# All loads of a fused attention and SwiGLU kernel moved to casting DMAs on GpSimd's queue, with the fp16 layout copies on VectorE

## The chip, the cores and the metric

One core of a Trainium2 chip. The metric is the time on the device of one execution, in microseconds (us). The kernel before took 395.26 us (median of three runs, 394.04 to 395.29). TensorE is called PE, VectorE DVE, ScalarE ACT, GpSimd POOL and SyncE SP in the profile.

## The reference

```python
# q, k, v: (8, 8, 576, 64) fp32: batch, heads, sequence, head size; window = 32
scores = where(|i - j| <= 32, q @ k.T / 8, -1e9)
attn_out = softmax(scores) @ v
x = attn_out.transpose(0, 2, 1, 3).reshape(4608, 512)
g = x @ w_gate                       # (512, 1536)
out = (silu(g) * (x @ w_val)) @ w_out # (1536, 512) -> (4608, 512) fp32
```

## The kernel before

The tokens are worked on in nine chunks of 512. `ffn1(j)` makes the gate and value products of chunk j in twelve units of eight matmuls (512 columns), and `ffn2` multiplies back in four pieces. Attention for the next batch is woven in: q and k are transposed inside `ffn1(j)`, scores and the products with V run between the pieces of `ffn2`. All orders are written by hand: the program sets the order in which each engine gets its instructions. I call `ffn1(j)` and `ffn2(j)` with batch j+1 "round j"; rounds 1 to 6 are alike, and the last two chunks have no attention beside them.

```python
def cast_qk(st, cast):                       # fp32 staging -> fp16, permuted
    t16 = qk16.tile([128, J9, 2, D], FP16, ...)
    cast(t16.rearrange("p j h d -> p h j d"), st.rearrange("p h (j d) -> p h j d", d=D))
    return t16

def transpose_qk(t16, pool=None):            # nine 128x128 transposes on TensorE
    ...
def place_q(src, b, half, hh, cast): ...     # copies PSUM -> qB, 64 partitions a time
def place_k(src, b, half, cast): ...         # copies PSUM -> kT

def ffn1_unit(j, fk):
    gv = ps_a.tile([128, 2, 512], FP32, tag="a", ...)   # ps_a has 2 buffers
    for i, w in enumerate((wg16, wv16)):
        for g in range(GS):
            nc.tensor.matmul(out=gv[:, i, :], lhsT=w[:, g, ...], rhs=xts[j][:, g, :], ...)
    nc.scalar.activation(out=ssb, in_=gv[:, 0, :], func=AF.Silu, ...)
    nc.vector.tensor_tensor(out=hts[j][:, fk, :], in0=ssb, in1=gv[:, 1, :], op=ALU.mult)  # hT

def ffn1(j):
    b = j + 1
    for u in range(FKS):                     # FKS = 12
        ffn1_unit(j, u)
        ...
        for step in {0: ("q0", "k0", "v0", "q1"), 2: ("v1",), 3: ("k1",), ...}.get(u, ()):
            # GpSimd: cast V pieces, or h16[step] = cast_qk(staged tile, cast_pool)
        if u in (1, 3, 5, 7):                # q at 1 and 5, k at 3 and 7
            ps = transpose_qk(h16[...])
            # q: place_q(ps, b, half, 0) on VectorE; k: place_k on ScalarE
        if u in (2, 6):
            place_q(ps, b, u // 4, 1, cast_dve)
        # SP: loads of q, k, V of batch b + 1 into fp32 staging tiles
```

In the profile `gv_ps` is the gate and value product in PSUM (where TensorE's results land), `ssb` silu of the gate, `hT` the product of both that `ffn2` reads, `qk_ps` the transposed q or k in PSUM and `o_ps` the product with V.

In `ffn2` each finished 128x512 tile of x is turned by a transposing DMA on SP (`pair_xt`) into `xT`, the input of the next `ffn1`.

## Time and profile before

| | before |
|---|---|
| time, us | 395.26 |
| span of the profiled run, us | 393.5 |
| start of the first `ffn1`, us | 30.5 |
| start of round 1, us | 78.1 |
| one round of 2 to 5: `ffn1` + `ffn2`, us | 25.8 + 14.3 or 15.3 |
| end of round 6, us | 325.2 |

The page's head and its slices (the busy share in tenths of 40 equal slices of the span; PEclk is TensorE's granted clock):

```profile
span 393.5 us, 6234 instructions
...
PE 352.8 (90%) x2490; PEld 182.5 (46%) x2490; DVE 191.4 (49%) x277; ACT 167.6 (43%) x226; POOL 115.3 (29%) x154
...
PE   2679997688999899988998899889988999999993
...
PEclk9999999589999999999999999999999999999998
```

TensorE is the bottleneck from the end of the prologue on. GpSimd's 115 us of casts are not: TensorE hardly waits for them. The table of stretches shows round 2, `ffn1` and then `ffn2` (columns: length, busy time of each engine, clock, share of the DMA engines, GB/s):

```profile
core 0: us, PE busy (x) PEld busy (x) DVE busy (x) ACT busy (x) POOL busy (x), PEclk, DMA share, GB/s
120.01:145.84 25.83, 23.50 (x141) 11.72 (x142) 12.82 (x15) 10.70 (x16) 11.21 (x15) 1.00 0.61 155
145.84:161.18 15.34, 15.34 (x164) 8.52 (x162) 8.65 (x16) 8.43 (x10) 1.23 (x2) 1.00 0.37 87
```

TensorE is idle for 2.3 us of that `ffn1` (25.83 less 23.50). The timeline of round 1 shows that it is not the q transposes that wait: they follow the matmuls of unit 1 at once, while VectorE is not yet done with the unit (columns: start, length, engine, line, operation, count, and in brackets the idle time before it):

```profile
82.00 1.03 PE L379 MATMUL gv_ps<-xT,wv_128 128*128 128x512 f16 x4
...
82.86 0.67 PE L276 MATMUL qk_ps<-ident,t_934 128*128 128x128 f16 x9
...
83.69 0.69 DVE L386 TENSOR_TENSOR hT<-ssb,gv_ps 128x512 f16<-128x512 f16 x1 [1.04 <-ACT ssb L385]
```

The chain of waits (start, length, what, followed back from the end) leaves TensorE only for the k transposes, which need the buffer that the second q copy still reads:

```profile
83.53 1.74 PE gv_ps L379 x8
...
85.92 0.69 DVE hT L386
86.61 0.03 issue
86.64 1.37 DVE qB_101 L259
88.02 0.14 issue
88.15 0.66 PE qk_ps L276 x9
```

Unit 3's matmuls had ended 1.17 us before 88.15. This happens twice a round, which makes the 2.3 us.

### The profile page before, as it was taken

The numbers are of one execution on the slowest core, as the hardware profiler recorded it, in microseconds if no ns is written. First come the engines' busy times: TensorE is split into PE (matmuls) and PEld (weight loads), VectorE is DVE, ScalarE is ACT, GpSimd is POOL, SyncE is SP. The second block draws the span as 40 slices with busy tenths as digits, with TensorE's granted clock in tenths as the row PEclk, the third lists the DMA queues.
The fourth block names the chain that finished last, engine by engine and source line by source line (L and its number), as shares of the span: only waits on it lengthen the run. The fifth ranks groups of instructions, "written<-read, shape, count | busy, mean of one in ns | idle before, by whom it ended". The sixth has DMA issues, their size and how long they took to land.

```text
span 393.5 us, 6234 instructions
## 1 busy us (share of the span) xinstructions
PE 352.8 (90%) x2490; PEld 182.5 (46%) x2490; DVE 191.4 (49%) x277; ACT 167.6 (43%) x226; POOL 115.3 (29%) x154
## 2 busy tenths in 40 slices
PE   2679997688999899988998899889988999999993
PEld 2544454444454445544544455445544544444441
DVE  6763565855364635454536544554365463412420
ACT  4614337433544346333733474436433644323321
POOL 5867470396501541056005610281000000000000
PEclk9999999589999999999999999999999999999998
DMA  8999942997048803690269015930400041011002
GB/s 267 251 373 382 340 109 92 306 285 124 2 94 273 155 2 82 195 259 1 71 179 272 2 60 105 315 60 27 135 0 2 27 108 40 2 53 55 0 28 86
DMA packets 73539, 51.33 MB, mean 130 GB/s; under 512 B 54048, under 2 KB 59168, under 8 KB 73504
## 3 DMA queue, kind: packets, MB, share of 16 engines
q1 hardware_dynamic: 73504, 50.87, 48.3%
q8 instruction: 21, 0.34, 0.4%
q14 instruction: 14, 0.11, 0.1%
HBM read 37.75 MB, written 9.44 MB: 120 GB/s over the span
## 4 chain that ended last, share of the span: by engine, by line
PE 81%; DVE 11%; ACT 4%; DMA 2%; issue 1%; SPq 0%; ACTq 0%
PE gv_ps L379 43%; PE ob L393 24%; PE qk_ps L276 5%; PE o_ps L342 4%; PE s_ps L304 4%; DVE hT L386 2%; DVE qB_101 L259 2%; DVE qB_102 L259 2%; ACT ssb L385 2%; DMA qk_st<-in_q_dram 2%; DVE p_t L313 2%; PE xt_ps L366 1%; ACT p_t L311 1%; DVE v_103 L259 1%; PE warm L409 1%
## 5 line engine op out<-in xcount | busy, mean ns | idle before, releaser
L386 DVE TENSOR_TENSOR hT<-ssb,gv_ps 128x512 f16<-128x512 f16 x108 | 74.3, 688 | 137.6 <-ACT ssb L385 137.2
L385 ACT ACTIVATE ssb<-gv_ps 128x512 f16<-128x512 f32 x108 | 64.5, 597 | 116.1 <-PE gv_ps L379 116.0
L379 PE MATMUL gv_ps<-xT,wg_127 128*128 128x512 f16 x432 | 111.7, 381 | 1.8 <-ACT xT L256 1.4
L379 PE MATMUL gv_ps<-xT,wv_128 128*128 128x512 f16 x432 | 111.4, 380 | 0.0
L393 PE MATMUL ob<-wo_129,hT 128*128 128x512 f16 x432 | 101.0, 379 | 0.0
L379 PEld LDWEIGHTS <-wv_128 128*128 128x128 f16 x432 | 42.5, 98 | 51.6 <-issue 1.1
L379 PEld LDWEIGHTS <-wg_127 128*128 128x128 f16 x432 | 41.3, 98 | 47.5 <-issue 3.5
L393 PEld LDWEIGHTS <-hT 128*128 128x128 f16 x432 | 40.0, 98 | 41.1
L311 ACT ACTIVATE p_t<-s_ps 128x1024 f16<-128x1024 f32 (+1 forms) x40 | 37.1, 938 | 18.8 <-PE s_ps L304 18.8
L313 DVE TENSOR_TENSOR p_t<-p_t,mask 128x1024 f16<-128x1024 f16 (+1 forms) x40 | 28.5, 719 | 30.2 <-ACT p_t L311 30.1
L401 ACT ACTIVATE osb<-ob 128x512 f32<-128x512 f32 x36 | 21.5, 597 | 50.2 <-PE ob L393 49.5
L262 POOL CAST v_103<-vS 64x512 f16<-64x512 f32 (+1 forms) x48 | 29.9, 623 | 20.5 <-issue 14.0
L262 POOL CAST v_104<-vS 64x512 f16<-64x512 f32 (+1 forms) x48 | 30.2, 630 | 6.6 <-DMA vS<-in_v_dram 4.4
L342 PEld LDWEIGHTS <-p_t 128*64 128x64 f16 x576 | 19.3, 119 | 14.9 <-issue 10.1
L259 DVE COPY qB_101<-qk_ps 64x1152 f16<-64x1152 f16 x16 | 21.6, 1353 | 2.2 <-PE qk_ps L276 2.0
L259 DVE COPY qB_102<-qk_ps 64x1152 f16<-64x1152 f16 x16 | 21.6, 1353 | 2.2 <-PE qk_ps L276 2.0
L304 PE MATMUL s_ps<-qB_101,kT_99 128*128 128x128 f16 x144 | 13.4, 239 | 3.5 <-ACT p_t L311 3.5
L304 PEld LDWEIGHTS <-kT_99 128*128 128x128 f16 x144 | 10.5, 107 | 6.9 <-issue 4.1
L342 PE MATMUL o_ps<-v_104,p_t 128*64 128x66 f16 x288 | 12.3, 205 | 0.7 <-DVE v_104 L259 0.7
L256 ACT ACTIVATE kT_99<-qk_ps 128x1152 f16<-128x1152 f16 x8 | 9.0, 1129 | 7.8 <-PE qk_ps L276 7.8
L349 DVE RECIPROCAL rall<-o_ps 128x8 f32<-128x8 f32 x36 | 7.5, 207 | 10.0 <-PE o_ps L342 8.4
L342 PE MATMUL o_ps<-v_103,p_t 128*64 128x66 f16 x288 | 12.2, 208 | 0.1
(193 smaller groups left out, 208.2 us busy)
## 6 DMA issues: line engine op xcount, KB each, us to landing
qk_st<-in_q_dram SPq DMA_DIRECT2D x16, 576.0 KB, 6.0
qk_st<-in_k_dram SPq DMA_DIRECT2D x16, 576.0 KB, 7.3
out_dram<-osb SPq DMA_DIRECT2D x36, 256.0 KB, 2.0
vS<-in_v_dram SPq DMA_DIRECT2D x24, 256.0 KB, 8.6
vS<-in_v_dram SPq DMA_DIRECT2D x16, 192.0 KB, 7.0
wost_t<-in_moe_w_out_dram SPq DMA_DIRECT2D x4, 768.0 KB, 8.8
wst_t<-in_moe_w_gate_dram SPq DMA_DIRECT2D x3, 768.0 KB, 8.5
wst_t<-in_moe_w_val_dram SPq DMA_DIRECT2D x3, 768.0 KB, 9.5
```

The source lines that it names most:

```text
L259: nc.vector.tensor_copy(out=o, in_=i)
L262: nc.gpsimd.tensor_copy(out=o, in_=i)
L276: nc.tensor.transpose(out=ps[:, 128 * j:128 * j + 128], in_=t16[:, j, :, :], identity=ident)
L304: nc.tensor.matmul(out=dst, lhsT=kT[b % 2][:, hp, 64 * t:64 * t + 128], rhs=qB[b % 2][:, hp, :, 64 * t:64 * t + 64], start=True, stop=True)
L311: nc.scalar.activation(out=p[:, :, f0:f1, :], in_=s, func=AF.Exp, bias=0.0, scale=1.0 / float(D) ** 0.5)
L313: nc.vector.tensor_tensor(out=p[:, :, f0:f1, :], in0=p[:, :, f0:f1, :], in1=mask[:, :, f0:f1, :], op=ALU.mult)
L342: nc.tensor.matmul(out=o[64 * i:64 * i + 64, h // 4, 66 * (h % 4):66 * (h % 4) + 66], lhsT=p[:, i, POS[h], :], rhs=v16[b % 2][:, t, h, :], ...
L379: nc.tensor.matmul(out=gv[:, i, :], lhsT=w[:, g, 128 * fk:128 * fk + 128], rhs=xts[j][:, g, :], start=(g == 0), stop=(g == GS - 1))
L385: nc.scalar.activation(out=ssb, in_=gv[:, 0, :], func=AF.Silu, bias=0.0, scale=1.0)
L386: nc.vector.tensor_tensor(out=hts[j][:, fk, :], in0=ssb, in1=gv[:, 1, :], op=ALU.mult)
L393: nc.tensor.matmul(out=ob, lhsT=hts[j][:, fk, 128 * sub:128 * sub + 128], rhs=wo16[:, fk, :], start=(fk == 0), stop=(fk == FKS - 1))
L401: nc.scalar.activation(out=osb, in_=ob, func=AF.Copy, bias=0.0, scale=1.0)
```

## The change

Its intent: no fp32 staging tiles and no casts on any engine. All loads become casting DMAs (transfers that turn fp32 into fp16 on the way), issued from GpSimd's software queue, that write V and the weights where they are used and q and k into a fp16 tile. The permutation of q and k that the cast did on the way becomes a fp16 copy on VectorE inside `transpose_qk`, and the odd key blocks of V are made from the even ones by two VectorE copies. The places in `ffn1` move too: transposes at units 1, 4, 6, 9.

```diff
     def load_qk(src, b, half):
-        st = qkst.tile([128, 2, J9 * D], FP32, tag="qkst", name="qk_st")
-        nc.sync.dma_start(out=st, in_=src[b, 4 * half:4 * half + 4].rearrange(
+        t16 = qk16.tile([128, 2, J9 * D], FP16, tag="qk16", name="t16")      # 8 buffers
+        nc.gpsimd.dma_start(out=t16, in_=src[b, 4 * half:4 * half + 4].rearrange(
             "(f h) (p j) d -> (h p) f (j d)", h=2, j=J9))
     # load_v, load_w_slab, load_wo likewise: nc.gpsimd.dma_start straight into fp16
-    def transpose_qk(t16, pool=None):
+    def transpose_qk(raw, pool=None):
+        t16 = qkp.tile([128, J9, 2, D], FP16, tag="qkp", name="t16p")        # 3 buffers
+        nc.vector.tensor_copy(out=t16.rearrange("p j h d -> p h j d"),
+                              in_=raw.rearrange("p h (j d) -> p h j d", d=D))
         ...
+    def shift_v(b, ms):                      # two VectorE copies, 64 partitions each
     # ---- ffn1(j), after ffn1_unit(j, u), for batch b = j + 1
+            if u in (3, 8):
+                shift_v(b, [0, 1] if u == 3 else [2, 3])
-            if u in (1, 3, 5, 7):
-                half = u // 4
-                ps = transpose_qk(h16[...])
+            if u in (1, 4, 6, 9):
+                half = u // 5
+                ps = transpose_qk(h16[...])
-            if u in (2, 6):
+            if u in (2, 7):
                 place_q(...)
-                for step in {3: ("q0", "k0"), 7: ("q1", "k1")}.get(u, ()):   # loads of b + 1
-                if u >= 7:
-                    load_v(b + 1, [u - 7])
+                if u == 1:
+                    load_qk_all(b + 1)
     # ---- ffn2(j), after a piece
+            if slot == 3 and j + 2 < B:
+                load_v(j + 2, range(5))
     # cut: all weight loads and batch 1's loads are issued at the start; the mask is built
     # from a 128x64 tile; fills of the V tile go to VectorE; two idle matmuls less
```

More of the change, by code (lines that the diff above doesn't have):

```diff
@@ L162 @@
     const = fast.enter_context(tc.tile_pool(name="const", bufs=1))
-    wst = fast.enter_context(tc.tile_pool(name="wst", bufs=5))
-    qkst = fast.enter_context(tc.tile_pool(name="qkst", bufs=4))
-    qk16 = fast.enter_context(tc.tile_pool(name="qk16", bufs=4))
+    qk16 = fast.enter_context(tc.tile_pool(name="qk16", bufs=8))
+    qkp = fast.enter_context(tc.tile_pool(name="qkp", bufs=3))
     ppool = fast.enter_context(tc.tile_pool(name="pp", bufs=5))
@@ L180 @@
     v16 = [const.tile([128, NT, H, 66], FP16, name=f"v16{i}") for i in range(2)]
-    vS = const.tile([128, 5, H, D], FP32)
     ident = keep.tile([128, 128], FP16)
@@ L195, in fill_fixed @@
             return
-        nc.gpsimd.memset(v16[i][:, :, :, 64:66], 1.0)
-        nc.gpsimd.memset(v16[i][0:32, 0, :, 64:66], 0.0)
-        nc.gpsimd.memset(v16[i][96:128, NT - 1, :, 64:66], 0.0)
+        eng.memset(v16[i][:, :, :, 64:66], 1.0)
+        eng.memset(v16[i][0:32, 0, :, :], 0.0)
+        eng.memset(v16[i][96:128, NT - 1, :, :], 0.0)
     masks.make_identity(nc, ident)
-    nc.gpsimd.memset(vS[0:32, 0, :, :], 0.0)
-    nc.gpsimd.memset(vS[96:128, 4, :, :], 0.0)
-    for part in range(4):
+    for part in (3, 0, 1, 2):
         fill_fixed(0, nc.vector, part)
-    nc.gpsimd.memset(mask, 1.0)
-    mk = mask.rearrange("p a h q -> p (a h) q")
-    nc.gpsimd.affine_select(out=mk, in_=mk, pattern=[[0, 2 * H], [-1, 64]], base=0,
+    mb = const.tile([128, 64], FP16)
+    nc.gpsimd.memset(mb, 1.0)
+    nc.gpsimd.affine_select(out=mb, in_=mb, pattern=[[-1, 64]], base=0,
                             channel_multiplier=1, compare_op=ALU.is_ge, fill=0.0)
-    nc.gpsimd.affine_select(out=mk, in_=mk, pattern=[[0, 2 * H], [1, 64]], base=64,
+    nc.gpsimd.affine_select(out=mb, in_=mb, pattern=[[1, 64]], base=64,
                             channel_multiplier=-1, compare_op=ALU.is_ge, fill=0.0)
+    nc.vector.tensor_copy(out=mask.rearrange("p a h q -> p (a h) q"),
+                          in_=mb.unsqueeze(1).to_broadcast([128, 2 * H, 64]))
     wg16 = keep.tile([128, GS, d_ff], FP16)
@@ L217, in load_qk, with load_w_slab @@
     def load_qk(src, b, half):
-        st = qkst.tile([128, 2, J9 * D], FP32, tag="qkst", name="qk_st")
-        nc.sync.dma_start(out=st, in_=src[b, 4 * half:4 * half + 4].rearrange(
+        t16 = qk16.tile([128, 2, J9 * D], FP16, tag="qk16", name="t16")
+        nc.gpsimd.dma_start(out=t16, in_=src[b, 4 * half:4 * half + 4].rearrange(
             "(f h) (p j) d -> (h p) f (j d)", h=2, j=J9))
-        return st
+        return t16
     def load_v(b, ms):
-        vb = v[b].rearrange("h s d -> s h d")
+        src, dst = v[b].rearrange("h s d -> s h d"), v16[b % 2]
         for m in ms:
             if m == 0:
-                nc.sync.dma_start(out=vS[32:128, 0, :, :], in_=vb[0:96])
+                nc.gpsimd.dma_start(out=dst[32:128, 0, :, 0:D], in_=src[0:96])
             elif m == 4:
-                nc.sync.dma_start(out=vS[0:96, 4, :, :], in_=vb[480:576])
+                nc.gpsimd.dma_start(out=dst[0:96, 8, :, 0:D], in_=src[480:576])
             else:
-                nc.sync.dma_start(out=vS[:, m, :, :], in_=vb[128 * m - 32:128 * m + 96])
+                nc.gpsimd.dma_start(out=dst[:, 2 * m, :, 0:D],
+                                    in_=src[128 * m - 32:128 * m + 96])
     slab0 = [sum(SLABS[:i]) for i in range(len(SLABS))]
-    def load_w_slab(w, s):
-        st = wst.tile([128, GS, SLABS[s]], FP32, tag="wst", name="wst_t")
-        nc.sync.dma_start(
-            out=st,
-            in_=w.rearrange("(g p) c -> p g c", p=128)[:, :, slab0[s]:slab0[s] + SLABS[s]])
-        return st
-    def cast_w_slab(st, w16, s, cast):
-        cast(w16[:, :, slab0[s]:slab0[s] + SLABS[s]], st)
+    def load_w_slab(w, w16, s):
+        cols = slice(slab0[s], slab0[s] + SLABS[s])
+        nc.gpsimd.dma_start(out=w16[:, :, cols],
+                            in_=w.rearrange("(g p) c -> p g c", p=128)[:, :, cols])
     def load_wo(s):
-        st = wst.tile([128, 3, d_model], FP32, tag="wst", name="wost_t")
-        nc.sync.dma_start(
-            out=st,
+        nc.gpsimd.dma_start(
+            out=wo16[:, 3 * s:3 * (s + 1), :],
             in_=moe_w_out.rearrange("(f p) c -> p f c", p=128)[:, 3 * s:3 * (s + 1), :])
-        return st
-    def cast_wo(st, s, cast):
-        cast(wo16[:, 3 * s:3 * (s + 1), :], st)
     def cast_act(o, i):
@@ L262, in cast_pool @@
         nc.gpsimd.tensor_copy(out=o, in_=i)
-    def cast_qk(st, cast):
-        t16 = qk16.tile([128, J9, 2, D], FP16, tag="qk16", name="t16")
-        cast(t16.rearrange("p j h d -> p h j d"),
-             st.rearrange("p h (j d) -> p h j d", d=D))
-        return t16
-    def transpose_qk(t16, pool=None):
+    def transpose_qk(raw, pool=None):
+        t16 = qkp.tile([128, J9, 2, D], FP16, tag="qkp", name="t16p")
+        nc.vector.tensor_copy(out=t16.rearrange("p j h d -> p h j d"),
+                              in_=raw.rearrange("p h (j d) -> p h j d", d=D))
         ps = (pool or ps_c).tile([128, 2048], FP16, tag="a" if pool is ps_a else "c",
@@ L286, in place_k @@
             "c a (p j) -> c a p j", j=J9), src)
-    def prep_v(b, m, ce, co1, co2):
-        vb = v16[b % 2]
-        if ce:
-            ce(vb[:, 2 * m, :, 0:D], vS[:, m])
-        if m < 4 and co1:
-            co1(vb[0:64, 2 * m + 1, :, 0:D], vS[64:128, m])
-        if m > 0 and co2:
-            co2(vb[64:128, 2 * m - 1, :, 0:D], vS[0:64, m])
+    def shift_v(b, ms):
+        vb, n = v16[b % 2], len(ms)
+        lo, hi = 2 * ms[0], 2 * ms[0] + 2 * n
+        nc.vector.tensor_copy(out=vb[0:64, lo + 1:hi:2, :, 0:D], in_=vb[64:128, lo:hi:2, :, 0:D])
+        nc.vector.tensor_copy(out=vb[64:128, lo + 1:hi:2, :, 0:D],
+                              in_=vb[0:64, lo + 2:hi + 1:2, :, 0:D])
     xts = {}
@@ L428, in check_range @@
         return flag
-    st, ws, h16 = {}, {}, {}
+    st = {}
     def load_qk_all(b):
@@ L439 @@
     load_v(0, range(5))
-    for s in range(3):
-        ws[("g", s)] = load_w_slab(moe_w_gate, s)
-        ws[("v", s)] = load_w_slab(moe_w_val, s)
-    c16 = [cast_qk(st[("q", 0)], cast_dve), cast_qk(st[("k", 0)], cast_act),
-           cast_qk(st[("q", 1)], cast_act), cast_qk(st[("k", 1)], cast_pool)]
+    for s in range(len(SLABS)):
+        load_w_slab(moe_w_gate, wg16, s)
+        load_w_slab(moe_w_val, wv16, s)
+    for s in range(4):
+        load_wo(s)
+    c16 = [st[("q", 0)], st[("k", 0)], st[("q", 1)], st[("k", 1)]]
+    load_qk_all(1)
+    load_v(1, range(5))
     t_q0 = transpose_qk(c16[0], ps_a)
@@ L455 @@
     place_k(t_k1, 0, 1, cast_act)
-    for m in range(3):
-        prep_v(0, m, cast_pool, cast_pool, cast_pool)
     quad_scores((2, 3), 0)
-    prep_v(0, 3, cast_dve, cast_dve, cast_dve)
+    shift_v(0, [0])
+    shift_v(0, [1])
     quad_scores((0, 1), 1)
-    prep_v(0, 4, None, None, cast_dve)
     quad_scores((2, 3), 1)
-    prep_v(0, 4, cast_pool, None, None)
-    for s in range(len(SLABS)):
-        if s >= 3:
-            ws[("g", s)] = load_w_slab(moe_w_gate, s)
-            ws[("v", s)] = load_w_slab(moe_w_val, s)
-        if s < 3:
-            cast_w_slab(ws[("g", s)], wg16, s, cast_pool)
-            cast_w_slab(ws[("v", s)], wv16, s, cast_pool)
+    shift_v(0, [2])
     idle_mms(3)
@@ L473 @@
     pair_av(1, ps_a)
+    shift_v(0, [3])
     pair_xt(0, True)
-    idle_mms(1)
     pair_av(2)
     pair_xt(1, True)
-    idle_mms(1)
     pair_av(3, ps_a)
@@ L482 @@
     pair_xt(3, True)
-    for s in range(4):
-        ws[("o", s)] = load_wo(s)
-    load_qk_all(1)
-    load_v(1, range(5))
     for u in range(FKS):
         ffn1_unit(0, u)
-        if u in (2, 4):
-            s = u // 2 + 2
-            cast_w_slab(ws[("g", s)], wg16, s, cast_pool)
-            cast_w_slab(ws[("v", s)], wv16, s, cast_pool)
-        if u >= 6 and u % 2 == 0 or u == 11:
-            n = (u - 6) // 2 if u < 11 else 3
-            cast_wo(ws[("o", n)], n, cast_pool)
         if u in (1, 3, 5, 7):
             fill_fixed(1, nc.vector, (u - 1) // 2)
-    c16 = [cast_qk(st[("q", 0)], cast_dve), cast_qk(st[("k", 0)], cast_pool),
-           cast_qk(st[("q", 1)], cast_dve), cast_qk(st[("k", 1)], cast_pool)]
+    c16 = [st[("q", 0)], st[("k", 0)], st[("q", 1)], st[("k", 1)]]
+    load_qk_all(2)
     ffn2_sub(0, 0)
@@ L518 @@
     ffn2_sub(0, 3, 1)
-    load_qk_all(2)
-    for m in range(3):
-        prep_v(1, m, cast_pool, cast_pool, cast_pool)
+    shift_v(1, [0, 1])
     pair_scores(6)
@@ L526 @@
     pair_av(5)
-    prep_v(1, 3, cast_dve, cast_dve, cast_dve)
+    shift_v(1, [2, 3])
     pair_scores(8)
@@ L530 @@
     pair_av(6)
-    prep_v(1, 4, None, None, cast_dve)
-    prep_v(1, 4, cast_pool, None, None)
     pair_av(7, ps_a)
@@ L545, in ffn1 @@
                 continue
-            for step in {0: ("q0", "k0", "v0", "q1"), 2: ("v1",), 3: ("k1",), 4: ("v2",),
-                         5: ("v3",), 6: ("v4",)}.get(u, ()):
-                n = int(step[1])
-                if step[0] == "v":
-                    prep_v(b, n, cast_pool, cast_pool, cast_pool)
-                else:
-                    h16[step] = cast_qk(st[(step[0], n)], cast_pool)
-            if u in (1, 3, 5, 7):
-                half = u // 4
-                ps = transpose_qk(h16[("q" if u % 4 == 1 else "k") + str(half)])
-                if u % 4 == 1:
+            if u == 0:
+                h16 = {"q0": st[("q", 0)], "k0": st[("k", 0)], "q1": st[("q", 1)],
+                       "k1": st[("k", 1)]}
+            if u in (3, 8):
+                shift_v(b, [0, 1] if u == 3 else [2, 3])
+            if u in (1, 4, 6, 9):
+                half = u // 5
+                ps = transpose_qk(h16[("q" if u in (1, 6) else "k") + str(half)])
+                if u in (1, 6):
                     place_q(ps, b, half, 0, cast_dve)
@@ L559, in ffn1 @@
                     place_k(ps, b, half, cast_act)
-            if u in (2, 6):
-                place_q(ps, b, u // 4, 1, cast_dve)
+            if u in (2, 7):
+                place_q(ps, b, u // 5, 1, cast_dve)
             if b + 1 < B:
-                for step in {3: ("q0", "k0"), 7: ("q1", "k1")}.get(u, ()):
-                    n = int(step[1])
-                    st[(step[0], n)] = load_qk({"q": q, "k": k}[step[0]], b + 1, n)
-                if u >= 7:
-                    load_v(b + 1, [u - 7])
+                if u == 1:
+                    load_qk_all(b + 1)
     for j in range(1, NCH):
```

## The prediction

> **What bounds it now.** TensorE. The page's busy row gives PE 90% of a 393.5 us span; the chain that ended last is 81% PE. By stages (windows table): the prologue, 0 to 30.5 us, is bound by the four 576 KB q/k loads and the scores behind them; the first FFN1 (30.5 to 51.5) is solid matmuls; six rounds of about 41 us start at 78 (PE busy 38.4 to 39.2 in each); the last 70 us have no attention work. GpSimd's 115 us are almost all off the chain. In the chain of waits each round loses PE time at two places only: the k transposes wait for the second q copy on VectorE (PE ends 85.27, silu 0.61, hT 0.69, q copy 1.37, transposes at 88.15: 1.17 us of PE idle).
>
> **What the change does.** It removes GpSimd casts (1.15 us per q/k tile) and the prologue's ACT and VectorE casts: little of it on the chain. It moves all loads from SP to GpSimd's software queue. The Trainium skill ("DMA: Bandwidth & Descriptors", SWDGE vs HWDGE vs iDMA) says a casting DMA must go there and that GpSimd's cores write its descriptors; no run shows the cost yet.
>
> It adds on VectorE: a 128x1152 fp16 permuting copy before each of the 32 transposes, and V shifts. The fp32-input cast took 1.16 to 1.26 us; a masked multiply of 128x1024 fp16 took 0.72; I estimate 0.5 to 0.8 from these.
>
> **The step I expect to decide.** Before, the permuted tile was made early on GpSimd, so q transposes followed the matmuls at once (82.86 in round 1). In the changed order of instructions VectorE runs hT(u), then the permuting copy, and PE runs unit u's matmuls, then at once the transposes of that copy. So PE must wait for silu + hT + copy: 0.61 + 0.69 + about 0.6 + some 0.25 of semaphores = about 2.1 us, four times a round (u = 1, 4, 6, 9), six rounds: 24 x 2.1 = 50 us. The old k wait goes (k is now two units after the q copy): 12 x 1.17 = 14 us back. Net +36 us. In batch 1's preparation k copies stand behind q copies (2 x 1.36 us) while PE has 1.3 us of other matmuls: +4 us; cheaper V work there: -1.
>
> **Prologue.** The first load starts about 1.3 us later; V pieces have 1024 runs of 256 B, and weights queue behind them in one in-order queue with at most eight loads in flight. If descriptors are cheap, the first FFN1 starts near 31; at some ns each (a guess) it starts 10 us or more late. I take +8. The skill ("SBUF — State Buffer", Who interferes with whom) says VectorE's two-port copies and descriptor writing block each other.
>
> **Sum.** 395.3 + 36 + 4 - 1 + 8 = about 442 us; range 418 to 475. Faster by over 2%: 0.03; within 2%: 0.04; slower: 0.93.
>
> **What would show it.** Right: rounds of about 47 us in place of 41; in the waits, PE on qk_ps waiting for VectorE's t16p about 24 times at about 2 us; first gate matmul between 31 and 45 us.
>
> **What would make it wrong.** Transposes found ready (near 400); a permuting copy much shorter or longer than 0.6 us; software descriptors so slow that V or weights come late in every round (above 475); or casting DMAs that free enough of the prologue to pay for the waits (below 418).

## The result

The changed kernel took 454.98 us (median of four runs, 450.9 to 457.06), the kernel before beside it 395.27. The ratio is 1.15 (95% interval 1.1413 to 1.1588). A ratio here is the mean time of one kernel's runs over that of the other's runs of the same rounds, so it is not quite the ratio of the medians. The time lies inside the range; the estimate was 13 us too low.

Its four runs lie 6.2 us apart, and the granted clock of the slower two was 0.96, of the fastest 0.971.

The page after: the span is 61.8 us longer, and the software queue has appeared.

```profile
span 455.3 us, 6097 instructions
...
PE 367.1 (81%) x2488; PEld 184.2 (40%) x2488; DVE 210.2 (46%) x341; ACT 165.4 (36%) x224; POOL 68.3 (15%) x95
...
PE   1589976867896889568896889686987788999994
...
PEclk9999988599999899899999899899998999999998
...
q0 software_dynamic: 53088, 18.88, 38.6%
```

To find the 61.8 us I cut both timelines at the first gate matmul of every `ffn1` and the first matmul of every `ffn2`:

| stretch, us | before | after | more |
|---|---|---|---|
| start to first `ffn1` | 30.5 | 33.7 | +3.2 |
| first `ffn1` | 20.9 | 20.9 | 0 |
| its `ffn2` and batch 1's attention | 26.7 | 31.0 | +4.3 |
| `ffn1` of rounds 1 to 6, sum | 156.3 | 200.5 | +44.2 |
| `ffn2` of rounds 1 to 6, sum | 90.8 | 100.6 | +9.8 |
| the rest | 68.3 | 68.6 | +0.3 |

The first row moves from run to run: with the same prologue, copy_early, v4_late, both and fill_waits started their first `ffn1` at 32.2 to 33.1 us, and before_k_later, with the old prologue, at 29.3. The rounds are steadier. So 44 of 62 us are in `ffn1`, and the 9.8 us in `ffn2` are not spread: rounds 2 and 4 took 21.4 and 18.6 us in place of 15.3, and the others at most 0.4 more. The table of stretches for round 2, and for one piece of its `ffn1`:

```profile
135.01:168.28 33.27, 25.57 (x141) 11.92 (x142) 16.17 (x23) 10.27 (x15) 0.00 (x0) 0.95 0.09 16
168.28:189.64 21.36, 15.57 (x163) 8.45 (x161) 8.65 (x16) 10.31 (x12) 7.79 (x10) 1.00 0.99 122
```

```profile
148.85:152.06 3.21, 3.21 (x12) 1.13 (x10) 0.00 (x0) 1.13 (x1) 0.00 (x0) 0.53 0.00 0
```

The first line has 7.7 us of TensorE idle where before had 2.3, and 2.1 us more of busy time. The third line says where most of the busy time comes from: for about 3.2 us behind a wait the clock was at half (0.53 is the mean of the stretch). The second line has the DMA engines at 0.99, where before had 0.37. VectorE is busy for 16.2 of 33.3 us, so it is not full.

The list of waits names the new waiters (us in total, times, longest):

```profile
PE qk_ps L262 <- DVE t16p L257: 62.0, 29, 7.0
...
DVE x_1718 L336 <- DMA xT<-x_1607: 4.4, 1, 4.4
```

The chain of waits in `ffn1` of round 2 answers to the one of before. The first group of transposes waits for silu, hT and the copy; the second also for the V shifts, which stand before hT of its unit, and for the second q copy ahead of them (`qB_99`, 144.21 to 145.57 us, cut here). From 143.49 us until the permuting copy ended VectorE was never idle for more than 0.04 us:

```profile
138.67 0.61 ACT ssb L370
...
139.30 0.69 DVE hT L371
139.99 0.38 DVE t16p L257
140.37 0.05 issue
140.42 0.68 PE qk_ps L262 x9
...
145.60 0.69 DVE hT L371
...
146.32 0.42 DVE v_101 L278
...
146.77 0.42 DVE v_101 L279
...
147.22 0.69 DVE hT L371
147.91 0.38 DVE t16p L257
148.29 0.05 issue
148.34 0.68 PE qk_ps L262 x9
```

The timeline gives TensorE's idle time before these two groups as 1.78 and 2.07 us, and the same again for the other two: 7.7 us in the round.

The timeline of GpSimd's issues explains rounds 2 and 4 (40.91 us in the bracket is how long GpSimd sat still, waiting for a matmul with V):

```profile
131.66 0.87 POOL L229 DMA_DIRECT2D v_100<-in_v_dram  x1 [1.06 <-PE o_ps L327]
173.44 0.78 POOL L227 DMA_DIRECT2D v_100<-in_v_dram  x1 [40.91 <-PE o_ps L327]
174.21 0.71 POOL L217 DMA_DIRECT2D t_1768<-in_q_dram  x1
174.91 0.71 POOL L217 DMA_DIRECT2D t_1770<-in_k_dram  x1
175.60 0.72 POOL L217 DMA_DIRECT2D t_1772<-in_q_dram  x1
176.30 0.73 POOL L217 DMA_DIRECT2D t_1774<-in_k_dram  x1
177.00 0.83 POOL L225 DMA_DIRECT2D v_101<-in_v_dram  x1
```

GpSimd issues in the order of the program here: nothing passed the load that waited. A batch has nine key blocks, so one pair of blocks lies across an even batch and the next, and the fifth V piece cannot be written over until that pair's products are done, a round after the other four. All later loads stand behind it. When it goes, four q/k loads and V follow in one burst, in the very stretch in which the transposing DMAs of x run. One of them took 11.7 us to land; before, the longest took 5.2. The next `ffn1` waits for it:

```profile
176.68 11.74 DMA xT<-x_1607
```

### The profile page after: what moved, and what is told of

It reads as the page before. It is cut to its first block, busy times and chain, and to the rows that moved or that the text cites. A ratio compares the mean times of both kernels' runs of the same rounds, so it can differ in the third digit from the quotient of the medians.

```text
span 455.3 us, 6097 instructions
## 1 busy us (share of the span) xinstructions
PE 367.1 (81%) x2488; PEld 184.2 (40%) x2488; DVE 210.2 (46%) x341; ACT 165.4 (36%) x224; POOL 68.3 (15%) x95
## 4 chain that ended last, share of the span: by engine, by line
PE 65%; DVE 18%; DMA 7%; ACT 5%; issue 3%; POOL 0%; POOLq 0%; ACTq 0%
PE gv_ps L364 35%; PE ob L378 17%; DVE hT L371 7%; PE qk_ps L262 5%; PE s_ps L289 4%; PE o_ps L327 3%; ACT ssb L370 3%; DVE t16p L257 3%; DMA xT<-x_1607 3%; DVE qB_99 L248 2%; DMA xT<-x_2466 2%; DVE qB_98 L248 2%; ACT p_t L296 1%; DMA xT<-x_1234 1%; DMA t_126<-in_q_dram 1%
## 5 line engine op out<-in xcount | busy, mean ns | idle before, releaser
L364 PE MATMUL gv_ps<-xT,wg_123 128*128 128x512 f16 x432 | 117.0, 395 | 9.2 <-issue 4.4
L364 PE MATMUL gv_ps<-xT,wv_124 128*128 128x512 f16 x432 | 116.3, 393 | 0.0
L378 PE MATMUL ob<-wo_125,hT 128*128 128x512 f16 x432 | 102.3, 383 | 0.0
L262 PE MATMUL qk_ps<-ident,t16p 128*128 128x128 f16 x288 | 23.8, 235 | 62.0 <-DVE t16p L257 62.0
L364 PEld LDWEIGHTS <-wg_123 128*128 128x128 f16 x432 | 42.3, 101 | 59.3 <-issue 14.3
L364 PEld LDWEIGHTS <-wv_124 128*128 128x128 f16 x432 | 43.5, 101 | 55.3 <-issue 7.5
L262 PEld LDWEIGHTS <-t16p 128*128 128x128 f16 x288 | 18.4, 105 | 76.1 <-DVE t16p L257 75.3
L298 DVE TENSOR_TENSOR p_t<-p_t,mask 128x1024 f16<-128x1024 f16 (+1 forms) x40 | 25.3, 638 | 34.5 <-ACT p_t L296 34.4
L227 POOL DMA_DIRECT2D v_100<-in_v_dram x4 | 3.3, 834 | 104.8 <-PE o_ps L327 104.8
L245 ACT ACTIVATE kT_96<-qk_ps 128x1152 f16<-128x1152 f16 x8 | 9.0, 1130 | 26.1 <-PE qk_ps L262 26.1
L245 ACT ACTIVATE kT_97<-qk_ps 128x1152 f16<-128x1152 f16 x8 | 9.0, 1130 | 16.4 <-PE qk_ps L262 16.4
L327 PE MATMUL o_ps<-v_101,p_t 128*64 128x66 f16 x288 | 12.2, 208 | 1.9 <-DVE x_1689 L336 1.4
L289 PEld LDWEIGHTS <-kT_96 128*128 128x128 f16 x144 | 10.5, 108 | 7.2 <-issue 4.1
```

Source lines behind the costliest of these rows:

```text
L245: nc.scalar.activation(out=o, in_=i, func=AF.Copy, bias=0.0, scale=1.0)
L262: nc.tensor.transpose(out=ps[:, 128 * j:128 * j + 128], in_=t16[:, j, :, :], identity=ident)
L289: nc.tensor.matmul(out=dst, lhsT=kT[b % 2][:, hp, 64 * t:64 * t + 128], rhs=qB[b % 2][:, hp, :, 64 * t:64 * t + 64], start=True, stop=True)
L298: nc.vector.tensor_tensor(out=p[:, :, f0:f1, :], in0=p[:, :, f0:f1, :], in1=mask[:, :, f0:f1, :], op=ALU.mult)
L327: nc.tensor.matmul(out=o[64 * i:64 * i + 64, h // 4, 66 * (h % 4):66 * (h % 4) + 66], lhsT=p[:, i, POS[h], :], rhs=v16[b % 2][:, t, h, :], ...
L364: nc.tensor.matmul(out=gv[:, i, :], lhsT=w[:, g, 128 * fk:128 * fk + 128], rhs=xts[j][:, g, :], start=(g == 0), stop=(g == GS - 1))
```

## The experiments

Theory 1: most of the loss is order. TensorE's transposes are placed right behind a unit's matmuls while their input is made only after that unit's hT; the waits also cost clock. Theory 2: the loss in `ffn2` comes from the burst of loads behind the fifth V piece. Rivals: the software queue and its casting DMAs are slow in themselves; GpSimd's descriptor writing and VectorE block each other; VectorE has too much to do. Six kernels were run, each in three rounds against the kernel before, and all gave correct results. Stage times are those of each kernel's profiled run.

### copy_early: the copy one unit earlier

```diff
         for u in range(FKS):
+            if b < B and u in (0, 3, 5, 8):
+                early = permute_qk(h16[{0: "q0", 3: "k0", 5: "q1", 8: "k1"}[u]])
             ffn1_unit(j, u)
 ...
-                ps = transpose_qk(h16[...])
+                ps = transpose_qk(None, t16=early)
```

> The changed kernel with one edit: in rounds 1 to 6 the permuting q/k copy is issued on VectorE one unit earlier (ahead of hT(u-1), not behind hT(u)); same instructions, same loads, same amount of VectorE work. Theory 1 (order: TensorE waits for silu + hT + copy, 1.8 to 2.1 us four times a round, and pays one 3.4 us stretch at half clock for it): FFN1 of a round falls from 33.3 to about 23 us, 6 x 10.3 = 62 us less, total about 393 us, no half-clock stretch inside the rounds. Rival A (the software queue itself is slow, or its descriptor writing and VectorE block each other): the loads are unchanged, so the time stays within 10 us of 455. Rival B (VectorE has too much work): the work is the same, so most of the loss stays.

Measured: 403.97 us, ratio to before 1.0242 (1.0203 to 1.0282): 51 us gained of the 62 expected. `ffn1` of rounds 1 to 6 sums to 147.1 us (200.5 in the changed kernel), and the transposes now follow at once:

```profile
128.54 1.03 PE L368 MATMUL gv_ps<-xT,wv 128*128 128x512 f16 x4
...
129.41 0.67 PE L266 MATMUL qk_ps<-ident,t16p 128*128 128x128 f16 x9
...
129.91 1.03 PE L368 MATMUL gv_ps<-xT,wg 128*128 128x512 f16 x4
```

```profile
125.94:149.56 23.62, 23.54 (x140) 11.76 (x141) 15.79 (x22) 9.83 (x15) 0.00 (x0) 1.00 0.13 22
149.56:170.45 20.89, 15.57 (x163) 8.44 (x161) 9.01 (x17) 10.31 (x12) 7.79 (x10) 1.00 0.92 124
```

TensorE is idle for 0.1 us of round 2's `ffn1`, with the same VectorE work (the first copy of the round now lies just before this stretch), and the clock holds. The rivals that put the loss on the queue or on VectorE's load fall for this part: neither was touched. The expected 62 us was too much because rounds 1, 3 and 5 took 25.3 to 25.7 us and not 23: rounds 3 and 5 begin behind the long `ffn2` waits (second line, unchanged), and round 1 behind the patchy stage of batch 1, so part of each ran at half clock.

### v4_late: the fifth V piece behind the next q/k loads

```diff
             if slot == 3 and j + 2 < B:
-                load_v(j + 2, range(5))
+                load_v(j + 2, range(4))
 ...
-            if b + 1 < B:
-                if u == 1:
+            if u == 1:
+                if b + 1 < B:
                     load_qk_all(b + 1)
+                if b > 2:
+                    load_v(b, [4])
```

> The changed kernel with one edit: the fifth V piece of a batch, whose buffer is free only after the pair that crosses two batches, is issued behind the next batch's q/k loads, so those no longer queue behind it. Theory 2 (in rounds 2 and 4 the four q/k loads burst out together with V in the FFN2 stage and hold up the transposing DMAs of x, up to 11.7 us to land): FFN2 of rounds 2 and 4 falls from 21.4 and 18.6 to about 15.3 us, total about 9 us less, 446 us; x transposes land in 5 us or less. Rival (V loads alone, or any software-queue load beside the transposes, do it): little or nothing is gained, 452 to 456.

Measured: 443.8 us, ratio 1.1217 (1.1153 to 1.1281), 11.2 us below the changed kernel. `ffn2` of rounds 2 and 4 took 16.1 and 15.3 us, and an x transpose at most 6.2 us to land. The q/k loads now go out one by one inside `ffn1`, and the V pieces alone share `ffn2`:

```profile
161.16 0.70 POOL L217 DMA_DIRECT2D t<-in_k_dram  x1 [7.23 <-DVE t16p L257]
170.50 0.80 POOL L227 DMA_DIRECT2D v<-in_v_dram  x1 [8.63 <-PE o_ps L327]
171.29 0.77 POOL L225 DMA_DIRECT2D v<-in_v_dram  x1
```

```profile
165.33:181.44 16.11, 15.50 (x163) 8.46 (x161) 8.64 (x16) 8.96 (x11) 4.20 (x5) 1.00 1.14 108
```

Theory 2 holds, and its rival (any load beside the transposes does it) falls: five V pieces are still there. The DMA share of this `ffn2` is even higher, 1.14 as the view counts it (last line), so the 0.99 above is not by itself the sign of the loss; what in the burst delays the transposes is not shown. The landings reached 6.2 us, above the 5 expected. Of the 13.1 us less span of the profiled run 8.1 are in `ffn2`; 3.4 are clock, since `ffn1` of rounds 2 and 3 ran without a half-clock stretch and took 31.58 and 31.57 us (33.3 in the changed kernel) with the same waits. In round 2 that is not the edit's doing: its waits fell otherwise into the windows of the clock (see fill_waits).

### both: the two edits together

The edits are those of the last two runs.

> Both edits together. If the two causes are separate and add, about 384 us (455 - 62 - 9); rounds of about 38 us. If the faster rounds bring the loads and the x transposes closer together, a little of the 9 stays lost: 388 to 393.

Measured: 392.53 us, ratio 0.9919 (0.9848 to 0.999). The gains add up: 455.0 less 51.0 and 11.2 is 392.8. The expected 384 was too low by what copy_early had already shown. The kernel with all its casting loads and copies is now level with the kernel before.

### fill_waits: the waits left as they are, but filled

```diff
             if u in (1, 4, 6, 9):
+                idle_mms(7)          # results unused
                 half = u // 5
```

> The changed kernel with one addition: seven matmuls of no use (about 1.5 us at full clock) on TensorE ahead of each of the 24 groups of transposes in the rounds, inside the wait for the copy (1.8 to 2.1 us). The wait itself stays. If the half-clock stretch of 3.4 us in each round comes from TensorE standing idle, the stretches inside FFN1 vanish and each round gets about 1.8 us shorter: 6 x 1.8 = 11 us, about 444 us, FFN1 of a round about 31.5 us. If the clock drops for another reason, or the filler ends later than the copy, the time stays at 455 or rises.

Measured: 448.85 us, ratio 1.1362 (1.1299 to 1.1425), 6 us gained of the 11 expected. Rounds 2, 4 and 6 took 31.58, 31.57 and 31.56 us for `ffn1`, 1.7 us less than 33.26, with the wait still there:

```profile
138.25 1.68 PE L394 MATMUL warm<-mask 128*128 128x512 f16 x7
...
140.19 0.68 PE L262 MATMUL qk_ps<-ident,t16p 128*128 128x128 f16 x9 [0.27 <-DVE t16p L257]
```

So the half clock comes from TensorE standing idle, and it costs 1.7 us in a round. Rounds 3 and 5 (32.9 and 33.3 us) still had a slow stretch, which lies behind the `ffn2` wait that this run left alone, and round 1 gained 0.4: hence 6 and not 11.

Three rounds alone would not show this, as v4_late had two at full clock with nothing filled. The clock records of the traces do. Within one run all changes of the granted clock lie whole multiples of 3.413 us apart (in the changed kernel at 149.06, 152.48, 190.02 and 251.46), so each run can be cut into windows of that length. I took those that lie wholly inside `ffn1` of the six rounds and start at full clock, in all eight traces. Half clock followed the six in which TensorE was busy for 0.39 or 0.40 of the time, and none of the 319 in which it was busy for 0.43 or more; in fill_waits the lowest is 0.84. Here are one window of round 2 of the changed kernel and two of round 4 of v4_late:

```profile
145.65:149.06 3.41, 1.34 (x13) 0.71 (x12) 2.54 (x5) 0.60 (x2) 0.00 (x0) 1.00 0.00 0
...
238.64:242.05 3.41, 1.46 (x14) 1.00 (x15) 1.82 (x4) 1.26 (x2) 0.71 (x1) 1.00 0.00 0
252.30:255.71 3.41, 1.34 (x14) 0.91 (x14) 1.97 (x5) 1.17 (x2) 0.71 (x1) 1.00 0.00 0
```

Half clock followed the first and the third. The second holds the same wait of 2.07 us, all but its first 0.12 us. So where the windows happen to fall decides whether a wait costs clock. The busy share is not the whole rule: in batch 1's stage half clock also followed windows of 0.47 (fill_waits) and 0.51 (both).

### all_moved: the same order for the first two batches

```diff
+    p_q0 = permute_qk(c16[0])
+    p_k0 = permute_qk(c16[1], cast_act)
+    p_q1 = permute_qk(c16[2], cast_act)      # p_k1 on VectorE, between two q copies
 ...
     for u in range(FKS):
+        if u >= 9:
+            pre.append(permute_qk(c16[u - 9]))   # batch 1's tiles, in the first ffn1
         ffn1_unit(0, u)
```

> The kernel of run both, and the same order for the first two batches: k0 and q1 of batch 0 are permuted on ScalarE, k1 ahead of the second q copy, and batch 1's copies are made during the first FFN1. If what is left of the loss there (prologue 3 us, batch 1's preparation and attention 4 us) is also order alone, the first FFN1 starts at about 30 and round 1 at about 77 us: about 385 us in all, 392.5 - 7. If it is the later start and slower landing of the casting loads, the prologue keeps 2 to 3 us of it: about 388. In neither case does it beat the kernel before with k later (378.5).

Measured: 382.99 us, ratio 0.9691 (0.9632 to 0.9751): 9.5 us below run both. The first `ffn1` starts at 30.8 us (32.8 in both) and round 1 at 77.3 (84.9). So the placing of the copies was nearly all of that loss too (their order, and in the prologue also that ScalarE made two of them), and the changed kernel's ingredients, in another order, are 3% faster than the kernel before.

### before_k_later: only the places of the transposes, in the kernel before

```diff
-            if u in (1, 3, 5, 7):
-                half = u // 4
+            if u in (1, 4, 6, 9):
+                half = u // 5
 ...
-            if u in (2, 6):
-                place_q(ps, b, u // 4, 1, cast_dve)
+            if u in (2, 7):
+                place_q(ps, b, u // 5, 1, cast_dve)
```

> The kernel before with one edit taken from the change: units 1, 4, 6, 9 for the transposes (1, 3, 5, 7 before), so k's transposes no longer wait for the second q copy. If that wait (1.17 us, 12 times) was real lost TensorE time, about 381 us (395 - 14), FFN1 of a round 23.3 to 23.5 us in place of 25.8. If TensorE would have waited elsewhere, within 3 us of 395.

Measured: 378.54 us, ratio 0.9586 (0.9551 to 0.9621), the fastest of all. `ffn1` of rounds 1 to 6 sums to 141.7 us (156.3 before): the old k wait was real TensorE time. Of the 16.1 us less span 14.6 are there; 1.2 are in the prologue, which the edit does not touch. Together with all_moved it answers what the change is worth here apart from order: with the transposes equally well placed, the kernel with hardware-queue loads and GpSimd casts is 4.5 us faster (378.5 against 383.0; the intervals of the two ratios to before don't overlap). Why is not settled, as the two differ in more than the queue. Of the difference in span of the two profiled runs (382.3 less 377.4) 1.4 us are in the prologue, 2.6 in `ffn1` and 1.6 in `ffn2` of the rounds; batch 1's stage gives 1.0 back.

## Why the prediction was right

- The step expected to decide did: the transposes waited for silu, hT and the copy, four times a round in six rounds. The sum said 24 x 2.1 us. The waits measured 1.78 and 2.07 us; the copy took 0.45 us, not 0.6, and the V shifts, which I had not put into this wait, made the k waits longer, with the second q copy ahead of them. copy_early shows the cause: moving the copy alone took 53 of 200 us out of the six `ffn1`.
- The old k wait went away, as said: "12 x 1.17 = 14 us back". before_k_later took 14.6 us out of the six `ffn1`.
- "Net +36 us" for the rounds was the term that was mis-sized: `ffn1` took 44.2 us more. In a round of 2 to 6 it is 7.43 us: 7.70 of waits less 2.34 of the old ones is 5.36; 1.7 is half clock, which the sum did not have and fill_waits shows (in rounds 3 and 5 it followed the waits of `ffn2`). The last 0.4 is there at full clock too (v4_late, round 2); I estimate that most of it is lost overlap: in the kernel before, the q transposes start 0.17 us before the modelled end of the matmuls (82.86 against 83.03), and twice a round they no longer do.
- The sum had no term for `ffn2`, which took 9.8 us more. I saw one in-order queue as a danger for the weights in the prologue only. It struck in the rounds, where the fifth V piece held back all later loads and let them go beside the x transposes. v4_late shows it.
- The prologue term was +8 and measured +3.2; batch 1's stage was +3 and measured +4.3. all_moved takes back 2.9 and 5.3 us (2.0 and 5.5 against run both) by the placing of the copies, so most of the prologue's loss was not the software queue, as I had reckoned.
- That the sum was only 13 us off is partly luck: the prologue was reckoned 4.8 us too high, which hid part of the 18 us by which the rounds were reckoned too low (8.2 in `ffn1`, 9.8 in `ffn2`).
- "Software descriptors so slow that V or weights come late" did not happen. In the timeline GpSimd needs 0.72 us to issue a q load and 0.88 for a V piece of 1024 rows.
- The blocking of VectorE's copies and GpSimd's descriptor writing, taken from the Trainium skill ("SBUF — State Buffer"), played no part in the rounds: all copies there took 0.45 us. But no GpSimd issue ran beside one of them in the trace, so the rounds do not test it. The same section's statement on VectorE instructions with two SBUF inputs beside a GpSimd instruction that reads SBUF agrees with the traces in the main: before, the seven 128x512 mask multiplies beside GpSimd's casts took 424 to 1251 ns, the one without a cast 411, and after, with no casts, all eight took 418 to 427 ns. It was not each one that was held up: two beside casts took 424 and 426 ns.
- The rounds were predicted at 47 us and measured 47.5 to 54.6; the first gate matmul came at 33.7, in the range of 31 to 45.

## What to carry to other kernels

When a copy moves to another engine, look at where it stands in that engine's order against the instruction that waits for it: the copy of 0.45 us cost waits of 1.8 to 2.1 us, because it stood behind work that itself waited for TensorE. In an in-order load queue, ask for each load when its buffer comes free, and put the load with the late buffer last. And try the harmless part of a change (here the new places of the transposes) in the old kernel by itself: it was worth 4%, and it was hidden in a change that lost 15%.

## What the Trainium skill lacked or had wrong

- "TensorE: Matmul & The Clock Gate", Part 1, says the clock falls to half after at least one idle window of about 3.4 us. Here no idle time inside `ffn1` of round 2 was longer than 2.07 us, and a stretch at half clock of about 3.4 us still followed; it cost 1.7 us. That the half clock comes from idleness, and is half, agrees (fill_waits; 0.53 over 148.85 to 152.06). The page says that the window is free-running, and the changes of the clock agree: they lie whole multiples of 3.413 us apart. What a window may hold and still count as idle is not in that table; inside `ffn1` here windows with TensorE busy for 0.40 of the time did and with 0.43 did not.
- "DMA: Bandwidth & Descriptors", SWDGE vs HWDGE vs iDMA, says that a cast during DMA must be issued from GpSimd (no run here tries another way), but not what it costs. In the DMA records of the two traces a packet with 2304 bytes read took a median of 93 ns as plain copy and 107 ns casting to 1152; packets of 256 bytes read, most of them V rows, took 22 ns plain and 32 casting. The casting ones also came from the other queue; no run here separates the two.
- The same page, Issuing engines are not separate DMA queues, says that all queues share 16 engines and interleave, which fits that SP's transposes of x landed late, after up to 11.7 us, beside GpSimd's loads. The section gives no figure for what the order of one issuing engine can cost: here a load whose buffer was not free held all later ones of GpSimd back for 40.9 us.
- "SBUF — State Buffer", Who interferes with whom, says that the one that comes second is blocked until the first has finished. Of the 32 permuting copies 30 took 0.44 to 0.46 us; the first two, in the prologue beside GpSimd's issues, took 0.77 and 0.75, but a third beside an issue took 0.45. The page has nothing that tells these apart, and no run here does.
